# Four one-bank PSUM tiles become one tile of four banks, copied out by one ScalarE instruction a unit

## The chip, the core and the metric

The kernel runs on one core of one Trainium2 chip. A core has five engines with an instruction queue each: TensorE (PE in the profile, with its weight loads shown as PEld), VectorE (DVE), ScalarE (ACT), GpSimd (POOL) and SyncE (SP). The last two mostly issue DMAs here. Matrix products land in PSUM, which has eight banks of 512 float32 per partition. Every queue runs in order, and an instruction that needs another engine's result waits on that engine's semaphore. The metric is the time of one execution on the device in microseconds (us); lower is better.

## What is computed

The reference is one block with two halves, on `x` of 2048 x 576. Everything that the change touches is in the first half, a long convolution whose kernel is made on the chip:

```
h = _layernorm(x) * (1 + ca) + sa
logdA = dt * A;  P = exp(logdA[:, :, None] * l)
K = einsum("dn,dnl,dn->dl", Cc, P, dB).real
y = irfft(rfft(pad(u)) * rfft(pad(K)))[:L] + u * Dskip
x = x + ga * y
h = _layernorm(x) * (1 + cb) + sb
x = x + gb * (z1 * (w_sp @ layernorm(z2) + b_sp)) @ w_out
```

The second half is a gated MLP with a 2048 x 2048 mixing product.

## The kernel before

**Two phases.** The convolution (`ssm`) fills about the first 340 us of the span, the first layer normalisation of the MLP follows, and from about 400 us on TensorE works through the MLP's products without a pause. The convolution works in small units, each a generator: a step issues some instructions and yields. `ORDER`, a list of 1336 steps such as `e30` or `z16` (a letter for the kind of unit, a number for which one), says which unit takes its next step. Instructions are tied to that order on every engine's queue: `Pin` passes each of them through `keep_in_program_order`.

**Units that matter here.** `M` (`mod_unit`) makes the modulation rows; `A` (`ln_half`, 16 units) forms the first transform of the normalised input in four banks and copies it to `st1o`; `e`, `t`, `p`, `k` make the convolution kernel for a group of channels (`e` writes tiles `et`, `t` writes `ft`, `p` writes `pg`, `k` writes `kab`); `1` (`k1_unit`, 36 units, steps such as `115` for unit 15) transforms it in two banks and copies it to the tiles shown as `k_a` and `k_b`; `u` transforms the input into `uu`; `z` (`z_unit`, 36 units) multiplies the two: its first instruction is a VectorE product that reads a bank directly (`zz<-pk,uu`); `v` (`v_unit`, 36 units) transforms back in two banks and copies to `v`; `y` forms the output rows, and its VectorE sum also reads a bank.

**PSUM.** Four banks belong to two tiles `ps` of two banks each. The other four are four tiles of one bank, `pk_a` to `pk_d`, handed out by `ps1()`; the digits of `PLAN["pk"]` say which tile each request gets. A unit that needs two or four banks asks two or four times, and copies each bank out with a ScalarE instruction of its own: 4 x 128x288 in `ln_half`, 2 x 128x256 in `k1_unit` and `v_unit`, 2 x 128x288 in `mod_unit`. TensorE may write a bank again as soon as the copy of that one bank has ended.

**Waits.** The framework keeps instructions apart by tile: an instruction waits for earlier ones, on other engines, that touched the same tile. With four separate tiles this is a wait by bank.

Of the kernel before, what the change touches and what calls it, by code (L numbers as in the profile page):

```python
# [9 lines left out]
F32 = mybir.dt.float32  # L10
# [3 lines left out]
AF = mybir.ActivationFunctionType  # L14
# [16 lines left out]
COPIED = set()  # L31
# [6 lines left out]
    "pk": "01230123230123012301230120123012301231023102310232102130213021302130213021302301230122301230123012312031203120"  # L38
        "31203120312031203103201320323012302310231023103210321031203120132012031231201230123012032012031203120321021021"
        "30230123013021032103210321321031021032130130213021320123120312012301230123023102310231032103210123012301230213"  # L40
        "021320312031230123012310312031203120312031320120312031203123013021300101010101010101010101010101010101010101",
# [13 lines left out]
B0 O0 O0 O0 O0 B2 O0 O0 O0 O0 B7 O0 B1 O0 O0 O0 B6 O0 O0 O0 O0 O0 O0 x0 O0 O0 O0 O0 P0 S0 O0 S0 B3 O0 O0 i2 O0 O0 O0 P0 M2 O0 O0 S0 S0 B4 P0 S0 O0 Q0 P0 e1 S0 M2 e1 i1 e0  # L55
P0 P0 g0 e1 e0 P0 e0 e1 P0 t1 t2 i0 g1 O0 M2 e0 P0 M1 t1 t2 t1 P0 P0 t0 w3 P0 M1 t0 M2 t1 t0 t2 M1 M0 M1 M0 t0 e2 j1 R1 P0 p1 M3 t2 M0 p1 M3 R0 e2 R3 e6 p1 M0 B5 e2 M0 e6
M3 w4 k1 e4 e2 P0 M3 k1 O0 P0 e3 11 p0 e4 11 e6 M4 M0 e5 p0 P0 p0 e6 S1 S1 p2 M4 k0 M4 p2 11 R2 p2 e5 k0 e5 S1 M0 M3 M0 P0 k2 M4 e5 M0 P0 t5 k2 A0 e3 A0 S1 A0 A0 A0 w5 t5
S1 e3 P0 e3 A0 t3 S1 A1 t5 A1 A1 r2 A1 P0 t3 R4 A1 t7 A0 R5 A1 A2 A2 O0 P0 t3 t3 A2 A2 t4 P0 A1 A2 A2 A3 p3 A2 A3 t5 P0 r3 A3 A3 t4 t4 j2 M4 10 10 e4 A3 A3 A3 e4 12 p3 12
e7 p3 e7 P0 e7 R7 t7 10 R6 P0 p5 S2 12 k3 e8 e7 O0 k3 e8 A4 S2 A4 S2 A4 e8 S2 A4 A4 A4 e8 p5 P0 A5 t4 A5 A5 P0 A5 p5 A5 p4 A5 t7 a4 A4 A5 t6 A6 A6 A6 p4 A6 t6 A6 p4 A6 t8
A7 A7 P0 t7 A7 A7 O0 k4 A6 P0 S2 A7 13 t6 p7 A7 k4 t8 p7 R9 14 13 O0 k5 P0 P0 a5 t6 14 14 t8 p7 Q1 13 t8 M5 x3 k7 P0 e11 R8 A7 k5 M5 S3 k7 S3 A8 A8 e11 R11 e9 A8 e10 e11  # L60
P0 e9 e11 P0 p6 S3 S3 A8 P0 A8 R10 t10 A8 e10 A9 t10 A9 A9 A9 p8 p8 r6 e10 A9 A9 t9 e10 t10 A10 A8 P0 A10 A10 A10 A9 t11 p6 A10 A10 17 P0 t10 M5 p6 17 k6 M5 p8 t11 t9 17
k6 A11 A11 r7 S3 t11 t11 e12 A11 A11 Q2 15 R13 A11 A11 A10 p11 k8 t9 15 15 R12 A11 k8 A12 p11 A12 e12 A12 p11 A12 e14 A12 t14 A12 A13 e14 p10 A13 t14 A13 R15 e9 p10 A13
p10 A13 R14 A13 e9 t14 A12 e12 t12 e12 A14 A14 t9 A14 t15 A14 A14 t12 A13 t14 A14 t12 A15 A15 t14 O0 O0 A15 e16 k10 P0 A15 P0 A15 16 A15 P0 O0 p9 t12 k11 16 M5 p9 A14 A15
p9 C0 16 t14 18 c1 k10 f0 18 110 k11 18 110 e14 U2 110 U1 U0 t15 p12 111 t15 111 z2 111 t15 u2 t16 p12 u2 U5 p12 u0 e14 k9 c0 z2 z2 u0 k9 t16 k12 U4 p14 u1 19 U14 t16 U7
e16 k12 e15 19 t16 19 U23 e13 e15 e15 e16 u1 e15 c3 u7 e16 e13 p14 u4 u7 e13 u4 p14 c2 p15 z1 z1 e13 t13 U29 v2 u14 U6 t16 v2 p15 z4 U10 u14 t13 u6 t13 p15 t18 k15 z4 u6
u5 t16 k15 z1 p16 t18 p16 u29 e18 u5 U15 v1 z0 t13 u29 t18 e17 X1 t18 v1 U3 e18 115 115 u10 v1 v2 z0 u10 z0 X3 p16 e17 115 k14 k14 u3 b1 e17 e22 u3 p13 U12 e22 t17 e17
e18 112 e18 p13 e22 z4 p13 112 t22 t17 v0 e22 t22 t22 z6 112 z6 v0 U13 t17 z5 v4 k13 v4 t22 t17 z5 114 Q3 z6 k13 v0 114 p17 u15 e19 p17 t22 v6 p17 t19 u15 k16 z5 t18 t19
v6 114 t18 113 p18 113 113 k16 z3 v5 z3 p18 v6 u13 k17 t19 t22 v5 p18 U11 z7 e20 t19 u13 116 k17 e19 U9 z7 p22 k18 116 u23 k18 116 117 e20 v4 117 e20 p22 117 z7 p22 e23
t20 v7 z3 u23 t20 v5 z15 t20 z15 U18 v7 u12 e23 t24 e20 b0 v7 t20 z15 e19 e23 e26 u12 v3 e19 e23 v15 e26 p19 v3 t23 v3 v15 z14 u9 z9 p19 t20 t23 U16 u9 z10 p19 z14 v15
u11 t24 z9 t20 z14 u16 t24 z9 t23 U19 u11 u16 t23 k19 v14 e24 U17 p20 k19 e21 v14 e24 v9 z10 p20 v9 k22 p23 u17 119 t26 e21 t21 u17 e24 119 U8 e26 p23 k22 119 p20 e24 p23  # L70
t21 e21 e26 e21 z12 122 v9 t24 z12 t26 k20 122 W1 122 t21 u8 k20 y1 t26 y1 t21 U20 z12 k23 120 W3 u8 t26 k23 t25 120 120 y1 t26 p21 v12 123 p21 v12 z8 u18 t26 v12 z10 123
123 t24 p21 u19 z8 u18 z11 t24 k21 u19 t25 e32 U24 z8 v14 t25 k21 t25 v8 p24 y3 e25 v8 U21 p24 u20 z11 y3 X0 U28 118 e32 p26 z13 v8 118 p26 118 u20 e25 v10 v10 t28 e28
z11 z13 p24 v11 W0 p26 e28 e25 e28 t30 v11 z13 y0 e28 121 e25 t28 121 t30 k26 k24 121 t28 e32 k26 k24 y0 e30 U31 e32 e30 v11 v13 t30 e27 e30 t28 v13 t30 z16 z20 p25 U25
z16 v13 e30 124 v10 u25 t30 y3 124 u28 124 z20 t30 z17 t27 t28 p25 z20 p25 z16 t27 u28 u25 v20 k25 z17 t28 p30 v20 v16 t27 k25 t31 W4 126 v16 t27 z17 X4 126 p30 y0 e27
z19 y4 u21 e29 126 z19 y4 u21 p30 U22 v20 e29 v17 v16 e27 e29 y4 e33 v17 p28 e27 e29 k30 t31 p27 p27 k30 z19 X7 e33 125 125 p27 X2 u31 z23 t29 125 u31 t31 v19 k27 W7 z23
v19 t29 130 p28 t31 y7 k27 W2 130 u24 y7 z21 t29 p28 W6 z21 e31 130 e34 k28 t29 e33 u24 p29 e31 z21 v17 e31 u22 k28 e33 p29 y2 y2 e31 e34 p29 v21 y7 t34 v19 e35 u22 128
v21 t34 128 k29 128 p31 k29 U26 127 e35 e34 t34 127 e35 z23 e35 v21 e34 t33 X6 t34 p31 127 t32 v23 p31 U30 v23 129 z22 129 129 z18 t33 z22 k31 z18 u30 z18 u26 t34 t34 t33
k31 u30 y6 u26 131 t32 t35 131 U33 v18 131 y2 v23 z22 p34 y6 t32 v22 v18 t33 U35 v22 y6 U27 z29 p34 t32 u27 p34 z27 u27 z29 U32 u33 X8 v22 t35 t32 u33 U34 k34 z27 p33 t35
v29 k34 v18 p33 t32 v29 z27 134 X5 p33 W8 134 z28 t35 134 u34 u35 u34 z28 v27 u35 p35 v28 v27 p35 k33 z24 W11 v29 p35 v28 z31 p32 z24 z31 k33 133 133 k35 k35 y8 p32 v31
y8 133 p32 v27 z26 k32 z24 v31 135 k32 z26 132 z26 135 135 132 v24 v28 132 v31 W5 z34 v24 v26 D0 z35 L2 v26 v24 z34 L4 y5 v34 z35 L9 v34 y5 y8 L3 z25 z30 y5 L7 v35 z25  # L80
z25 u32 v35 u32 v25 z30 v25 L10 X19 L13 X11 v30 v26 L0 X17 X12 v25 z32 v30 L11 L20 v30 z33 z32 v32 X9 z33 v32 v33 v33 v34 W9 L12 L6 L1 v32 L14 v33 X13 y11 X10 X16 W13 y11
v35 y9 y13 W12 W10 W14 y12 L15 W16 y10 y13 L8 W17 L18 y12 y11 X14 W15 X15 W18 y9 y9 W19 y10 L19 y16 y16 y17 L22 y14 X18 y17 y15 y19 y18 y14 y12 y10 y15 y19 L16 y15 L17
y18 y16 y13 y17 y19 y14 y18
# [112 lines left out]
class Rings:  # L196
# [7 lines left out]
    def __call__(self, pool, shape, dt, name, bufs):  # L204
        if name not in self.plan:
            return pool.tile(shape, dt, name=name, bufs=bufs)
        if name not in self.tiles:
            self.tiles[name] = [pool.tile(shape, dt, name=f"{name}_{chr(97 + i)}", bufs=1) for i in range(bufs)]
        i = self.at[name]
        self.at[name] = i + 1  # L210
        return self.tiles[name][self.plan[name][i]]


class Pin:
# [5 lines left out]
    def __getattr__(self, name):  # L220
        f = getattr(self.engine, name)

        def call(*a, **k):
            return self.tc.keep_in_program_order(f(*a, **k))  # L224

        return call

# [9 lines left out]
def ssm(tc, I, x1_d, consts_s, dram, mod_d, mlp):  # L237
# [6 lines left out]
    with ExitStack() as ctx:  # L244
# [12 lines left out]

        def ps1():
            return ring(psp, [128, 512], F32, "pk", 4)
# [178 lines left out]
        def mod_unit(k):  # L438
            wm = wmt.pop(k)
            pm = [ps1(), ps1()]  # L440
            for hh in range(2):
                for kt in range(6):
                    j = (kt + 2 * hh) % 4
                    T.matmul(pm[hh][32 * j:32 * j + 32, :HC], ec[:, kt:kt + 1].to_broadcast([96, 32]),
                             wm[hh][:, kt], start=kt < 4, stop=kt >= 2, skip_group_check=True)
            yield
            mpart = ep.tile([128, D], F32, name="mpart", bufs=1)
            for hh in range(2):
                A.activation(v3(mpart)[:, hh], pm[hh][:, :HC], AF.Copy)
            yield  # L450
            pm = [ps1(), ps1()]
            for hh in range(2):
                T.matmul(pm[hh][:, :HC], ones, mpart[:, HC * hh:HC * hh + HC], start=True, stop=True)
            yield
            src = [t[:, :HC] for t in pm]
            if k == 2:
                for hh in range(2):
                    A.activation(v3(gar)[:, hh], src[hh], AF.Copy)
            elif k == 1:
                for hh in range(2):  # L460
                    V.scalar_tensor_tensor(v3(cga)[:, hh], src[hh], 1.0, v3(gar)[:, hh], op0=ALU.add, op1=ALU.mult)
# [2006 lines left out]
```

## Time and profile before

| | |
|---|---|
| median of three runs | 1696.31 us (1691.14 to 1697.28) |
| profiled execution | 1691.0 us, of which the span from first to last instruction is 1688.9 us |
| ScalarE in the span | 873.8 us busy, 1307 instructions |
| VectorE in the span | 1298.4 us busy, 2241 instructions |
| granted TensorE clock | 0.99 on average |

The page gives busy times by engine, the share of each engine in 40 slices, the DMA queues, the chain of work that ended last and the costliest groups. For a change in one stage the table by windows (busy time of each engine between two moments) and the timeline (each instruction with its start and length) say more than the page's averages. A row of the timeline reads: start, length, engine, line, operation, output<-input, partitions x elements; in brackets how long the engine had been idle before it and what ended that.

### The profile page before, as it was taken

What the parts mean: (1) busy time and instruction counts of PE and PEld (TensorE: products, weight loads), DVE (VectorE), ACT (ScalarE), POOL (GpSimd) and SP (SyncE); (2) the same over time, 40 slices, a digit from 0 to 9 for tenths busy, and PEclk for the clock granted to TensorE, in tenths of its full rate; (3) what the DMA queues carried; (4) which work ended last, traced back from release to release, by engine and by line L of the source; (5) the groups of instructions that cost most, each with busy time, mean ns of one, the idle gap of its engine ahead of it and who ended that gap; (6) DMA issues with size and microseconds to landing.
All of it is one profiled execution on the core that took longest, in us unless ns stands there. A gap on an engine that the chain in (4) does not pass through costs nothing.

```text
span 1688.9 us, 39922 instructions
## 1 busy us (share of the span) xinstructions
PE 1615.6 (96%) x16868; PEld 1235.7 (73%) x16868; DVE 1298.4 (77%) x2241; ACT 873.8 (52%) x1307; POOL 209.7 (12%) x340
## 2 busy tenths in 40 slices
PE   3778999989999999999999999999999999999999
PEld 1344677755555557778878888888888888888887
DVE  7898999867989877988997776894443487787555
ACT  6889999675776664555444433342321133353221
POOL 3251111112222110000000000000111100111100
PEclk9978999999999999999999999999999999999999
DMA  9667645596888898776738887664667573777560
GB/s 231 170 215 229 203 140 176 171 317 208 280 287 243 251 261 297 242 270 234 249 118 302 282 292 257 219 218 166 232 213 243 189 221 121 275 281 252 189 241 29
DMA packets 186402, 380.61 MB, mean 225 GB/s; under 512 B 38464, under 2 KB 105792, under 8 KB 185456
## 3 DMA queue, kind: packets, MB, share of 16 engines
q1 hardware_dynamic: 145216, 182.10, 35.2%
q0 software_dynamic: 34528, 169.11, 30.1%
q10 hardware_dynamic: 6480, 26.86, 3.9%
q8 instruction: 132, 2.16, 0.5%
q14 instruction: 46, 0.38, 0.1%
HBM read 272.73 MB, written 105.29 MB: 224 GB/s over the span
## 4 chain that ended last, share of the span: by engine, by line
PE 77%; DVE 7%; DMA 3%; issue 2%; ACT 2%; SPq 0%; POOL 0%; ACTq 0%; DVEq 0%; POOLq 0%
PE ps L224 58%; PE pz L224 10%; PE pk_b L224 2%; PE pk_a L224 2%; DMA zset<-set_d 2%; PE pk_c L224 2%; PE pk_d L224 1%; DVE zset L224 1%; DVE gt L224 1%; DVE bsz L224 1%; PE ps_a L224 0%; PE ps_b L224 0%; DMA v_d<-v_a 0%; PE pt L224 0%; DMA uu_a<-in_x 0%
## 5 line engine op out<-in xcount | busy, mean ns | idle before, releaser
L224 PEld LDWEIGHTS <-zset 128*128 128x128 f16 x7182 | 702.2, 98 | 86.5 <-DMA zset<-set_d 2.0
L224 PE MATMUL ps<-wsp,zset 128*128 128x256 f16 x6048 | 666.8, 273 | 2.2 <-DMA zset<-set_d 1.1
L224 PE MATMUL pz<-wz,nt 128*128 128x512 f16 (+1 forms) x1120 | 220.8, 358 | 1.5 <-ACT nt L224 1.0
L224 ACT ACTIVATE z<-gt 128x1024 f16<-128x1024 f32 x56 | 59.0, 1054 | 250.4 <-DVE gt L224 250.4
L224 PEld LDWEIGHTS <-nt 128*128 128x128 f16 x1120 | 109.4, 98 | 107.1 <-ACT nt L224 1.5
L2164 POOL DMA_DIRECT2D zset<-set_d x96 | 50.8, 529 | 862.5 <-PE ps L224 619.7
L224 PE MATMUL ps<-wout,z 128*128 128x288 f16 x1092 | 138.4, 286 | 0.0
L224 DVE SCALAR_TENSOR_TENSOR gt<-ps,sc,bsp 128x512 f32<-128x512 f32 x36 | 27.0, 749 | 143.0 <-PE ps L224 141.3
L224 PEld LDWEIGHTS <-z 128*128 128x128 f16 x1176 | 115.1, 98 | 28.9
L224 DVE TENSOR_TENSOR raw<-raw 128x256 f32<-128x256 f32 (+3 forms) x238 | 126.8, 539 | 7.7 <-DMA raw<-z_d 3.5
L224 PE MATMUL ps<-n2o,zset 128*128 128x256 f16 x1134 | 128.2, 273 | 0.0
L224 DVE SCALAR_TENSOR_TENSOR gt<-ps,sc,gt 128x512 f32<-128x512 f32 (+1 forms) x180 | 122.2, 696 | 7.6
L224 ACT ACTIVATE zset<-raw 128x1792 f16<-128x1792 f32 x48 | 81.1, 1691 | 59.3 <-PE ps L224 21.6
L224 DVE TENSOR_TENSOR zset<-raw,zset 128x1792 f16<-128x1792 f32 x48 | 96.9, 2020 | 15.7 <-ACT zset L224 15.7
L224 DVE TENSOR_TENSOR z<-ps,z 128x512 f32<-128x512 f32 (+1 forms) x126 | 72.0, 599 | 32.3 <-ACT z L224 25.9
L224 ACT ACTIVATE z<-pz,sc 128x512 f32<-128x512 f32 (+1 forms) x96 | 51.9, 574 | 39.9 <-PE pz L224 32.7
L224 ACT ACTIVATE wsp<-raw,sc 128x1792 f16<-128x1792 f32 x25 | 44.5, 1783 | 46.2 <-DVE raw L224 40.2
L224 ACT ACTIVATE z<-z,sc 128x1024 f32<-128x1024 f32 x21 | 24.1, 1148 | 76.0 <-DVE z L224 72.3
L224 ACT ACTIVATE z1b<-gt 128x512 f16<-128x512 f32 (+1 forms) x22 | 17.7, 821 | 84.0 <-DVE gt L224 84.0
L224 PE MATMUL ps<-n2q,wf 128*128 128x512 f16 x252 | 55.7, 379 | 0.0
L224 DVE BATCH_NORM_STATS2 bsz<-z 128x6 f32<-128x384 f32 x96 | 48.4, 548 | 5.0 <-ACT z L224 4.4
L224 DVE SCALAR_TENSOR_TENSOR wsp<-raw,sc,wsp 128x1792 f16<-128x1792 f32 x25 | 52.0, 2078 | 0.3 <-ACT wsp L224 0.3
(793 smaller groups left out, 2772.0 us busy)
## 6 DMA issues: line engine op xcount, KB each, us to landing
zset<-set_d POOLq DMA_DIRECT2D x96, 896.0 KB, 5.2
raw<-z_d SPq DMA_DIRECT2D x48, 512.0 KB, 5.6
set_d<-zset ACTq DMA_DIRECT2D x24, 896.0 KB, 6.4
z_d<-z POOLq DMA_DIRECT2D x32, 576.0 KB, 8.2
zset<-wa_d POOLq DMA_DIRECT2D x18, 896.0 KB, 4.9
raw<-in_w_spT SPq DMA_DIRECT2D x25, 512.0 KB, 4.4
set_d<-zset SPq DMA_DIRECT2D x12, 896.0 KB, 5.8
wst<-in_w_in SPq DMA_DIRECT2D x8, 1024.0 KB, 9.3
```

The source lines that it names most:

```text
L224: return self.tc.keep_in_program_order(f(*a, **k))
L2164: self.nc.gpsimd.dma_start(o, self.set_d[f, j - 1] if j else self.wa_d[f])
```

## The change

The four tiles become one tile `banks` of 128 x 4 x 512. `ps1()` returns one bank of it, and a new `psn(n)` returns n neighbouring banks. `PLAN["pk"]` is a new list of digits, so that a unit's banks lie side by side. Each unit of two or four banks then issues one copy for all of them. This takes 130 ScalarE instructions away (48 in `ln_half`, 36 each in `k1_unit` and `v_unit`, 10 in `mod_unit`) and 2 VectorE ones. The lines of `ORDER` are wrapped at other places, but its 1336 steps are the same. TensorE's, GpSimd's and SyncE's instructions and their order are the same too.

One tile for all four banks would make the framework keep every reader of `banks` apart from every writer. `Pin.apart` takes that back between TensorE and the two readers: for each product written, and each read, it declares that there is no dependence on recent accesses by the other side to other banks. `READS` holds the reads of both ScalarE and VectorE, and `WRITES` those of TensorE. Between a read by ScalarE and a read by VectorE nothing is declared.

```
+    def apart(self, done, aps):
+        b = {x for ap in aps for x in banks_of(ap)}
+        if b:
+            names = {ap.tensor.name for ap in aps if hasattr(ap, "tensor")} - {ap.tensor.name for ap in aps if banks_of(ap)}
+            ins = getattr(done, "ins", done)
+            mine, others = (WRITES, READS) if self.engine is self.tc.nc.tensor else (READS, WRITES)
+            for c, i, n in others:
+                if not b & c and not names & n:
+                    self.tc.declare_no_dep(ins, i, reason="another bank")
+            mine.append((b, ins, names))
+        return done
...
+READS, WRITES = deque(maxlen=48), deque(maxlen=320)
...
+        banks = psp.tile([128, 4, 512], F32, name="banks", bufs=1)
+
         def ps1():
-            return ring(psp, [128, 512], F32, "pk", 4)
+            return banks[:, ring.take("pk")]
+
+        def psn(n):
+            i = min([ring.take("pk") for _ in range(n)])
+            return banks[:, i:i + n]
...
         def ln_half(k):
-            pms = [ps1() for _ in range(4)]
+            pms = psn(4)
...
-            for g, pm in enumerate(pms):
-                A.activation(o[:, g], pm[:, :HC], AF.Copy)
+            A.activation(o, pms[:, :, :HC], AF.Copy)
+            for _ in range(4):
                 yield
...
         def k1_unit(g):
-            pm = [ps1(), ps1()]
+            pm = psn(2)
...
-            for h in range(2):
-                pk = pm[h][:, :256].rearrange("p (c k) -> p k c", c=8)
-                if (g, h) in COPIED:
-                    V.tensor_copy(o[:, :, h], pk)
-                else:
-                    A.activation(o[:, :, h], pk, AF.Copy)
-                yield
+            A.activation(o, pm[:, :, :256].rearrange("p h (c k) -> p k h c", c=8), AF.Copy)
+            yield
+            yield
...
         def v_unit(n):
-            pm = [ps1(), ps1()]
+            pm = psn(2)
...
-            for q in range(2):
-                A.activation(v[:, 256 * q:256 * q + 256], pm[q][:, :256], AF.Copy)
+            A.activation(v.rearrange("p (q d) -> p q d", q=2), pm[:, :, :256], AF.Copy)
```

What this makes of the queues shows at three places. The first is ScalarE's queue in the first stage, where `ln_half` unit 3 is copied to `st1o_b` and the first `k1` units to `k_a`. Before, the four copies of a unit are taken apart by other work:

```order
L224 ACTIVATE st1o_b<-pk_c 128x288
L224 ACTIVATE st1o_b<-pk_d 128x288
L224 ACTIVATE ft_b<-ps_b 128x1024
L224 ACTIVATE k_a<-pk_c 128x32x8
L224 ACTIVATE st1o_b<-pk_b 128x288
L224 ACTIVATE st1o_b<-pk_a 128x288
L224 ACT_TABLE_LOAD
L224 ACTIVATE et_a<-pk_c 128x512
L224 ACTIVATE k_a<-pk_b 128x32x8
L224 ACTIVATE et_d<-ps_b 128x1024
L224 ACTIVATE k_a<-pk_d 128x32x8
```

The same place in the changed kernel:

```order
L227 ACTIVATE st1o_b<-banks 128x1152
L227 ACTIVATE ft_b<-ps_b 128x1024
L227 ACTIVATE k_a<-banks 128x32x16
L227 ACT_TABLE_LOAD
L227 ACTIVATE et_a<-banks 128x512
L227 ACTIVATE k_a<-banks 128x32x16
L227 ACTIVATE et_d<-ps_b 128x1024
```

The whole copy stands where the first part stood, and the later parts have moved ahead of what stood between.

The second place is ScalarE's queue where, in the profiled execution of before, about 260 us have passed: the second half of `e30` (`et_e`), a load of a function table, `k1` unit 24 (`k_b`). Each row names the semaphores it waits for: `PE_49`, `DVE_49` and `Activation_49` count the instructions that those engines have ended, `DMASW` and `DMAHW` the DMAs. Before:

```order
L224 ACTIVATE et_e<-ps_b 128x1024 [waits DVE_49,PE_49]
L224 ACTIVATE v_a<-pk_a 128x256 [waits DMASW5_49,PE_49,Activation_49]
L224 ACTIVATE v_a<-pk_c 128x256 [waits DVE_49,PE_49,Activation_49]
L224 ACTIVATE et_e<-pk_b 128x512 [waits PE_49]
L224 ACT_TABLE_LOAD
L224 ACTIVATE ft_a<-ft_a 128x1024 [waits DVE_49]
L224 ACTIVATE k_b<-pk_c 128x32x8 [waits PE_49]
L224 ACTIVATE k_b<-pk_b 128x32x8 [waits PE_49]
L224 ACTIVATE ft_a<-ft_a,consts_s 128x1024
```

In the changed kernel:

```order
L227 ACTIVATE et_e<-ps_b 128x1024 [waits PE_49]
L227 ACTIVATE v_a<-banks 128x512 [waits DMASW5_49,PE_49,Activation_49]
L227 ACTIVATE et_e<-banks 128x512 [waits DVE_49]
L227 ACT_TABLE_LOAD
L227 ACTIVATE ft_a<-ft_a 128x1024
L227 ACTIVATE k_b<-banks 128x32x16 [waits PE_49]
L227 ACTIVATE ft_a<-ft_a,consts_s 128x1024
```

The two halves of `v_a` and of `k_b` have become one row each, and the second row of `et_e` waits for VectorE now. By the count that it waits for, the awaited instruction is the product of unit `z16` (`zz_a<-banks,uu_f`), which reads bank 2; `et_e` reads bank 3.

The third place is VectorE's queue at the same time, with the products of units `z16` and `z20`. Before:

```order
L224 TENSOR_TENSOR pg_a<-et_a,ft_b 128x1024 [waits PE_49]
L224 TENSOR_TENSOR zz_a<-pk_d,uu_f 128x1024 [waits PE_49,Activation_49]
L224 TENSOR_TENSOR zz_b<-pk_a,uu_b 128x1024 [waits PE_49,Activation_49]
L224 TENSOR_TENSOR pg_a<-et_a,ft_b 128x1024
L224 TENSOR_TENSOR zz_b<-zz_b 128x256 [waits DVE_49]
```

In the changed kernel:

```order
L227 TENSOR_TENSOR pg_a<-et_a,ft_b 128x1024 [waits PE_49]
L227 TENSOR_TENSOR zz_a<-banks,uu_f 128x1024 [waits PE_49,Activation_49]
L227 TENSOR_TENSOR zz_b<-banks,uu_b 128x1024 [waits Activation_49]
L227 TENSOR_TENSOR pg_a<-et_a,ft_b 128x1024
L227 TENSOR_TENSOR zz_b<-zz_b 128x256 [waits DVE_49]
```

The rows stand as before, but the counts differ. Before, `z20` waited for an earlier copy out of its own bank; now it waits for the whole copy of `k_b` above, which reads banks 1 and 2, while `z20` reads bank 0. Over the whole program 34 such waits of ScalarE for a VectorE read of another bank, and 35 of VectorE for a ScalarE read of another bank, are in the changed kernel, and none in the kernel before. All but four stand among the `z` and `y` units, from about 160 us on. TensorE waits for ScalarE at 185 places where it did at 333 (counting its accesses to these banks), always for a reader of the same bank or tile.

More of the change, by code (lines that the diff above doesn't have):

```diff
@@ L1 @@
 import math
+from collections import deque
 from contextlib import ExitStack
@@ new lines @@
+v12 123 p21 v12 z8 u18 t26 v12 z10 123 123 t24 p21 u19 z8 u18 z11 t24 k21 u19 t25 e32 U24 z8 v14 t25 k21 t25 v8 p24 y3 e25 v8 U21 p24 u20 z11 y3 X0 U28 118 e32 p26 z13
+v8 118 p26 118 u20 e25 v10 v10 t28 e28 z11 z13 p24 v11 W0 p26 e28 e25 e28 t30 v11 z13 y0 e28 121 e25 t28 121 t30 k26 k24 121 t28 e32 k26 k24 y0 e30 U31 e32 e30 v11 v13
+t30 e27 e30 t28 v13 t30 z16 z20 p25 U25 z16 v13 e30 124 v10 u25 t30 y3 124 u28 124 z20 t30 z17 t27 t28 p25 z20 p25 z16 t27 u28 u25 v20 k25 z17 t28 p30 v20 v16 t27 k25
@@ L84 @@
+v34 z35 L9 v34 y5 y8 L3 z25 z30 y5 L7 v35 z25 z25 u32 v35 u32 v25 z30 v25 L10 X19 L13 X11 v30 v26 L0 X17 X12 v25 z32 v30 L11 L20 v30 z33 z32 v32 X9 z33 v32 v33 v33 v34
+W9 L12 L6 L1 v32 L14 v33 X13 y11 X10 X16 W13 y11 v35 y9 y13 W12 W10 W14 y12 L15 W16 y10 y13 L8 W17 L18 y12 y11 X14 W15 X15 W18 y9 y9 W19 y10 L19 y16 y16 y17 L22 y14 X18
+y17 y15 y19 y18 y14 y12 y10 y15 y19 L16 y15 L17 y18 y16 y13 y17 y19 y14 y18
 """
@@ L208, in __call__, with take @@
             self.tiles[name] = [pool.tile(shape, dt, name=f"{name}_{chr(97 + i)}", bufs=1) for i in range(bufs)]
+        return self.tiles[name][self.take(name)]
+    def take(self, name):
         i = self.at[name]
         self.at[name] = i + 1
-        return self.tiles[name][self.plan[name][i]]
+        return self.plan[name][i]
 class Pin:
@@ L223, in call, with banks_of @@
         def call(*a, **k):
-            return self.tc.keep_in_program_order(f(*a, **k))
+            return self.apart(self.tc.keep_in_program_order(f(*a, **k)), a + tuple(k.values()))
         return call
+    def apart(self, done, aps):
[10 more added lines that the diff above has]
+READS, WRITES = deque(maxlen=48), deque(maxlen=320)
+def banks_of(ap):
+    t = getattr(ap, "tensor", None)
+    if t is None or not t.name.startswith("banks"):
+        return ()
+    at = {ap.offset % 2048}
+    for step, n in list(ap.ap)[1:]:
+        at = {o + step * j for o in at for j in (range(n) if step >= 512 else (0, n - 1))}
+    return {o // 512 for o in at}
 class Pinned:
@@ L447, in mod_unit @@
             mpart = ep.tile([128, D], F32, name="mpart", bufs=1)
+            A.activation(v3(mpart), pm[:, :, :HC], AF.Copy)
+            yield
+            pm = psn(2)
             for hh in range(2):
-                A.activation(v3(mpart)[:, hh], pm[hh][:, :HC], AF.Copy)
+                T.matmul(pm[:, hh, :HC], ones, mpart[:, HC * hh:HC * hh + HC], start=True, stop=True)
             yield
-            pm = [ps1(), ps1()]
-            for hh in range(2):
-                T.matmul(pm[hh][:, :HC], ones, mpart[:, HC * hh:HC * hh + HC], start=True, stop=True)
-            yield
-            src = [t[:, :HC] for t in pm]
+            src = pm[:, :, :HC]
             if k == 2:
-                for hh in range(2):
-                    A.activation(v3(gar)[:, hh], src[hh], AF.Copy)
+                A.activation(v3(gar), src, AF.Copy)
             elif k == 1:
-                for hh in range(2):
-                    V.scalar_tensor_tensor(v3(cga)[:, hh], src[hh], 1.0, v3(gar)[:, hh], op0=ALU.add, op1=ALU.mult)
+                V.scalar_tensor_tensor(v3(cga), src, 1.0, v3(gar), op0=ALU.add, op1=ALU.mult)
             elif k == 0:
-                for hh in range(2):
-                    V.tensor_tensor(v3(sga)[:, hh], src[hh], v3(gar)[:, hh], op=ALU.mult)
+                V.tensor_tensor(v3(sga), src, v3(gar), op=ALU.mult)
                 yield
@@ L473, in mod_unit @@
                 mrow = mpart if k == 4 else ep.tile([128, D], F32, name="gar", bufs=1)
-                for hh in range(2):
-                    if k == 4:
-                        A.activation(v3(mrow)[:, hh], src[hh], AF.Identity, bias=one)
-                    else:
-                        A.activation(v3(mrow)[:, hh], src[hh], AF.Copy)
+                if k == 4:
+                    A.activation(v3(mrow), src, AF.Identity, bias=one)
+                else:
+                    A.activation(v3(mrow), src, AF.Copy)
                 yield
@@ L548, in ln_half @@
                         rows = slice(32 * g, 32 * g + 32)
-                        T.matmul(pms[g][64 * t:64 * t + 64, :HC], x[rows], y[rows, c], start=st, stop=not st, skip_group_check=True)
+                        T.matmul(pms[64 * t:64 * t + 64, g, :HC], x[rows], y[rows, c], start=st, stop=not st, skip_group_check=True)
                 yield
             o = ring(ep, [128, 4, HC], F32, "st1o", 2)
-            for g, pm in enumerate(pms):
-                A.activation(o[:, g], pm[:, :HC], AF.Copy)
+            A.activation(o, pms[:, :, :HC], AF.Copy)
+            for _ in range(4):
                 yield
@@ L660, in k1_unit @@
                         s = slice(64 * h, 64 * h + 64)
-                        T.matmul(pm[h][64 * ri:64 * ri + 64, 64 * i:64 * i + 64], kk[s, i], r1[ri][s, s], start=True, stop=True,
+                        T.matmul(pm[64 * ri:64 * ri + 64, h, 64 * i:64 * i + 64], kk[s, i], r1[ri][s, s], start=True, stop=True,
                                  skip_group_check=True)
@@ L750, in v_unit @@
                     rows = slice(64 * q, 64 * q + 64)
-                    T.matmul(pm[q][:, :256], m[rows], zz[rows, k, 256 * r:256 * r + 256], start=not t, stop=t == len(terms) - 1,
+                    T.matmul(pm[:, q, :256], m[rows], zz[rows, k, 256 * r:256 * r + 256], start=not t, stop=t == len(terms) - 1,
                              skip_group_check=True)
```

70 lines of the change are left out of this document (31 added, 39 removed).

## Prediction

> **What bounds the kernel now.** I read the windows first, since one stage alone is changed, then the timelines of the two engines that empty PSUM.
>
> ```profile
> core 0: us, PE busy (x) PEld busy (x) DVE busy (x) ACT busy (x) POOL busy (x), PEclk, DMA share, GB/s
> 60.00:158.00 98.00, 75.42 (x1695) 41.31 (x1693) 89.08 (x165) 90.62 (x183) 39.37 (x62) 0.83 0.63 196
> 158.00:335.00 177.00, 171.97 (x3960) 126.39 (x3960) 170.40 (x218) 159.53 (x279) 25.90 (x43) 1.00 0.59 176
> ...
> 340.00:360.00 20.00, 16.69 (x202) 13.54 (x198) 14.45 (x34) 14.74 (x25) 3.29 (x6) 1.00 1.08 335
> ...
> 400.00:450.00 50.00, 50.00 (x271) 26.46 (x269) 46.65 (x142) 35.97 (x57) 11.04 (x15) 1.00 0.74 228
> ```
>
> From 400 us on TensorE is full and nothing of its work changes, so whatever the convolution gains or loses moves the end by as much. From 60 to 158 us ScalarE (92%) and VectorE (91%) lead; from 158 to 335 us three engines are nearly full: TensorE idles 5.0 us of 177, VectorE 6.6, ScalarE 17.5. From 340 us the DMA engines are full. A stage with so little idle time gains little when one engine is relieved, and loses at once when one engine is held.
>
> **Fewer copies.** The timeline of ScalarE shows what a copy costs in a row of copies:
>
> ```profile
> 208.47 0.38 ACT L224 ACTIVATE k_a<-pk_c 128x256 f32<-128x256 f32 x1
> 208.75 0.38 ACT L224 ACTIVATE k_a<-pk_a 128x256 f32<-128x256 f32 x1
> 209.02 0.60 ACT L224 ACTIVATE uu_h<-pk_b 128x512 f32<-128x512 f32 x1
> 209.49 1.05 ACT L224 ACTIVATE ft_b<-ps_a 128x1024 f32<-128x1024 f32 x1
> 210.40 0.42 ACT L224 ACTIVATE v_a<-pk_c 128x256 f32<-128x256 f32 x1
> 210.66 0.44 ACT L224 ACTIVATE v_a<-pk_a 128x256 f32<-128x256 f32 x1
> ```
> ```profile
> 100.45 0.39 ACT L224 ACTIVATE st1o_b<-pk_a 128x288 f32<-128x288 f32 x1
> 100.74 0.40 ACT L224 ACTIVATE st1o_b<-pk_c 128x288 f32<-128x288 f32 x1
> ```
>
> A 128x256 copy lasts about 0.40 us, but the next begins 0.26 us after its start: their ends overlap. A 128x512 one takes the queue for 0.47 us and a 128x1024 one, across two banks, for 0.91. That is 0.84 ns for an element and some 0.045 us for an instruction. Two copies of 256 made one save 0.05 us, and four of 288 (0.29 each, 1.16) against one of 1152 (0.045 + 0.97 = 1.01) save 0.15. So 72 x 0.047 + 16 x 0.15 + 10 x 0.05 gives 6.3 us of ScalarE: 3.8 before 158 us (`ln_half`, `mod_unit` and half of `k1_unit`) and 2.5 after. By lengths (four 0.43 us copies against one of about 1.15, two of 0.40 against 0.61, two of 0.42 against 0.67) it would be 24.5 us, the upper bound; the lower is nothing. I take 6.3, the distance of starts being what a full queue pays. The Trainium skill ("ScalarE: Activation LUTs", What ACT_TABLE_LOAD costs) gives 186 ns + 0.833 ns an element, and about 93 ns of overlap: 130 x 0.093 = 12 us. The length of 0.40 agrees; the overlap here is 0.13 us, so I stay with the rows. Of the 3.8 us before 158 us I let half reach the end, as VectorE is as full: **-2** (0 to -3.8). The 2.5 after it go into the next part.
>
> **Copies that hold banks longer.** TensorE's waits from 60 to 158 us show that banks are short there:
>
> ```profile
> PE pk_a L224 <- ACT st1o_b L224: 2.4, 2, 1.8
> PE pk_c L224 <- ACT st1o_b L224: 2.2, 3, 1.3
> ```
>
> The first bank of an `ln_half` unit came free after 0.43 us and will after 1.15, 0.72 later, 16 times: 0 to +11.5 us. The last comes free 0.15 earlier (1.30 against 1.15), and in this stage TensorE idles a quarter of the time and ScalarE has other work in its queue. I take 0. The other end stays in the range. The new digits of the plan leave as many steps between a copy and the next use of its bank as before or more, so I count nothing for them.
>
> **New waits between ScalarE and VectorE.** This decides. In the changed program a copy by ScalarE waits for the VectorE read of `banks` that stands ahead of it in the list of steps, and a VectorE read for the copy ahead of it, whatever the banks: 34 and 35 waits that did not exist. They cost nothing where the two queues pass these points in the order of the list, but the list was free to run them past each other. The place at 260 us:
>
> ```profile
> 261.50 0.62 ACT L224 ACTIVATE et_e<-pk_b 128x512 f32<-128x512 f32 x1
> 262.14 1.28 ACT L224 ACT_TABLE_LOAD   x1
> 263.43 1.06 ACT L224 ACTIVATE ft_a<-ft_a 128x1024 f32<-128x1024 f32 x1
> 264.39 0.37 ACT L224 ACTIVATE k_b<-pk_c 128x256 f32<-128x256 f32 x1
> 264.66 0.38 ACT L224 ACTIVATE k_b<-pk_b 128x256 f32<-128x256 f32 x1
> ```
> ```profile
> 262.56 1.22 DVE L224 TENSOR_TENSOR zz_a<-pk_d,uu_f 128x1024 f32<-128x1024 f32 x1 [1.65 <-PE pk_d L224]
> 263.70 1.22 DVE L224 TENSOR_TENSOR zz_b<-pk_a,uu_b 128x1024 f32<-128x1024 f32 x1
> 264.84 1.22 DVE L224 TENSOR_TENSOR pg_a<-et_a,ft_b 128x1024 f32<-128x1024 f32 x1
> ```
>
> `et_e` began at 261.50, and now has to wait for the end of `z16` at 263.78: +2.28. Behind it stand the table load, `ft_a` and `k_b`, which moves from 264.39 to 266.67 and, 0.61 long, ends at 267.28. `z20` began at 263.70 and now waits for that: +3.58 on VectorE, with `pg_a` and all later products queued behind it. So each engine holds the other in turn.
>
> I compared start and end at each crossing of the two timelines from `z2` to the last `y` before 341 us. In 32 of them the awaited instruction ended after the waiting one had begun: 17 on VectorE, 17.9 us in sum, and 15 on ScalarE, 23.4 us. The first and the last before 335 us:
>
> ```profile
> 160.38 1.22 DVE L224 TENSOR_TENSOR zz_a<-pk_a,uu_a 128x1024 f32<-128x1024 f32 x1
> ...
> 332.52 1.23 DVE L224 TENSOR_TENSOR zz_b<-pk_b,uu_h 128x1024 f32<-128x1024 f32 x1 [2.10 <-PE pk_b L224]
> ```
> ```profile
> 161.34 0.60 ACT L224 ACTIVATE et_c<-pk_b 128x512 f32<-128x512 f32 x1
> ...
> 333.90 0.38 ACT L224 ACTIVATE kab_b<-pk_c 128x256 f32<-128x256 f32 x1 [1.83 <-PE pk_c L224]
> ```
>
> They are 161.94 - 160.38 = 1.56 and 334.28 - 332.52 = 1.76 us. The sums overlap, since a late engine no longer has to wait for the other; so I carried two delays, a for ScalarE and d for VectorE, from crossing to crossing: where VectorE waits, d becomes at least a plus the shortfall there, and where ScalarE waits, a at least d plus its own. At the last crossing before 335 us d is 31 us if neither catches up, and 18 if every idle moment of both (the 17.5 and 6.6 us above) goes into catching up. The first is too much, the second too little, because most idle moments were waits for TensorE, which comes later too when its inputs do. I take the middle, 24.5, less the 2.5 us that ScalarE saves there: **+22** (15 to 31).
>
> **The tail.** From 340 us on loads of `v_d` and of the MLP's weights share full DMA engines.
>
> ```profile
> wst<-in_w_in SPq DMA_DIRECT2D x2, 1024.0 KB, 11.4
> ```
>
> Weight loads need none of the late results. If they get out of the way in time, the last stretch is shorter: those 2 MB and 1 MB in smaller ones take 10 us at the 335 GB/s of the row at 340 us. They stand in one queue with loads that have to wait, so I take **-4** (0 to -10).
>
> **Sum.** -2 + 0 + 22 - 4 = +16 us on the profiled execution's 1691.0, 1707. The median of the runs shown stands 5.3 us above it, so I predict 1712. 0.5% of it is 8.5 us, about what a measurement can tell from no change.
>
> **Rivals.** *The waits are absorbed.* If the relieved ScalarE runs ahead and the crossings fall into the list's order by themselves, only the two savings remain, -2 to -6, and the tail cannot shrink: about 1692. For it: ScalarE has 17.5 us idle and the waits reorder the queues only by 1 to 3 us. Against it: VectorE has 6.6 us idle and is held 17.9 by starts alone. 0.17.
>
> *ScalarE is the bound and instructions cost their length.* Then up to 24.5 us leave its queue, but VectorE's work stays and it idles 8.9 + 6.6 us from 60 to 335 us, so at most some 13 us reach the end: 1683 to 1687. Against it stand the overlapping starts. 0.05.
>
> *TensorE slows down as well.* The windows show its clock at 0.83 where it was 77% busy and at 1.00 where it was 97% busy. With 22 us more, the stage to 335 us would be 86% busy, between these; at 0.92 its 172 us would take 15 us more: about 1727. 0.14. The Trainium skill ("TensorE: Matmul & The Clock Gate", What's actually happening) halves the clock after an idle window of about 3.4 us; single holds here are 1 to 3.6 us. By that rule the cost would come in pieces, as the rows above, a mean of 0.83, allow.
>
> *The copies are not the changed thing*, because the one tile makes TensorE wait for other banks too: its waits point to readers of its own bank, so 0.02, and about 1735.
>
> **How the numbers follow.** The forecast has 0.62, with 1703 to 1722 as its own range. The range reaches down to the sum of the low ends (15 - 3.8 - 10 = +1, 1697) and up into the slower clock, with the held banks: 1697 to 1731. Slower by over 0.5% is above 1704.8: nearly all of the forecast and the two slow rivals, 0.77. Below 1687.8: the second rival and a little of the first, 0.06. Between: 0.17.
>
> **What would show it.** Right: ScalarE's instructions fall by 130 but its busy time by 5 to 10 us only; rows of `zz` and `xb` on VectorE with ScalarE as the releaser of the idle time, and copies (`et`, `uu`, `v`, `k`) on ScalarE with VectorE as theirs, some 30 us in all between 160 and 340 us, where before there was almost none; the `z` stage 15 to 25 us longer, and the MLP as long as before. Wrong: the two waits for each other sum to a few us, or the first stage to 158 us changes by more than 5 us either way, or the MLP from 400 us on changes its length.

## The result and the profile after

The changed kernel takes 1737.72 us (median of four, 1735.83 to 1740.60) against 1696.80 before: a ratio of 1.0249, 95% interval 1.0222 to 1.0277. The forecast of slower was right and its size was not: +41 us by medians where +16 was predicted. The profiled execution took 1735.8 us, 44.8 more than that of before, of which the span is 1733.9.

| | before | changed |
|---|---|---|
| ScalarE busy, instructions | 873.8 us, 1307 | 870.4 us, 1177 |
| VectorE busy, instructions | 1298.4 us, 2241 | 1300.0 us, 2239 |
| granted TensorE clock | 0.990 | 0.980 |
| first `z` product starts | 160.38 us | 169.78 us |
| last crossing of the prediction (`zz_b` of `uu_h`) starts | 332.52 us | 374.67 us |

The same two VectorE instructions that the prediction quoted as the first and the last of their stage, in the timeline of the changed kernel:

```profile
169.78 1.23 DVE L227 TENSOR_TENSOR zz_a<-banks,uu_a 128x1024 f32<-128x1024 f32 x1 [1.83 <-ACT et_c L227]
...
374.67 1.22 DVE L227 TENSOR_TENSOR zz_b<-banks,uu_h 128x1024 f32<-128x1024 f32 x1 [5.80 <-ACT kab_b L227]
```

So, of the 44.8 us between the two profiled executions, 9.4 were lost ahead of the `z` units, 32.8 more between the two instructions (called the `z` stage from here on), and from there to the end 2.7. The windows of the changed kernel, cut at these two instructions (start:end, length, busy time of each engine with its instructions, granted clock, DMA share, GB/s):

```profile
60.00:169.78 109.78, 79.43 (x1757) 46.09 (x1752) 90.65 (x167) 89.73 (x121) 38.53 (x60) 0.77 0.60 187
169.78:374.67 204.89, 175.79 (x3844) 125.25 (x3844) 167.69 (x212) 154.72 (x220) 24.93 (x43) 0.97 0.49 144
```

And before, cut at the same two instructions:

```profile
60.00:160.38 100.38, 77.55 (x1715) 42.39 (x1713) 91.42 (x168) 92.98 (x187) 39.37 (x62) 0.83 0.64 199
160.38:332.52 172.14, 167.58 (x3822) 123.34 (x3822) 165.93 (x212) 156.23 (x272) 24.11 (x42) 1.00 0.59 174
```

VectorE does the same 212 instructions in the second stretch and is busy for as long (167.7 against 165.9 us), but the stretch is 32.8 us longer: VectorE waits. TensorE's busy time grows by 8.2 us (for 3844 matmul records against 3822) with its clock at 0.97. The waits of the changed kernel from 160 to 380 us (engine, tile written, awaited engine and tile: us in total, times, longest), VectorE's first:

```profile
DVE zz_b L227 <- ACT k_b L227: 5.8, 2, 3.5
DVE zz_b L227 <- ACT kab_b L227: 5.8, 1, 5.8
...
DVE zz_a L227 <- ACT v_a L227: 4.1, 2, 2.9
DVE xb_a L227 <- ACT kab_b L227: 3.1, 2, 2.2
```

ScalarE's, from the same view:

```profile
ACT kab_b L227 <- DVE zz_b L227: 4.0, 1, 4.0
ACT v_a L227 <- DVE zz_b L227: 3.2, 1, 3.2
ACT v_b L227 <- DVE zz_b L227: 2.7, 2, 2.5
ACT v_a L227 <- DVE zz_a L227: 2.4, 1, 2.4
ACT et_e L227 <- DVE zz_a L227: 2.3, 1, 2.3
```

Summed over all rows of the view, VectorE waits 32.2 us for ScalarE there (7.6 in the same window of before, of which 0.6 lie in the `z` stage of before) and ScalarE 28.6 for VectorE (0.6 before). The place at 260 us that the prediction worked out lies at 285 us now:

```profile
285.93 0.60 ACT L227 ACTIVATE et_e<-banks 128x512 f32<-128x512 f32 x1 [2.26 <-DVE zz_a L227]
286.55 1.28 ACT L227 ACT_TABLE_LOAD   x1
287.84 1.06 ACT L227 ACTIVATE ft_a<-ft_a 128x1024 f32<-128x1024 f32 x1
288.80 0.58 ACT L227 ACTIVATE k_b<-banks 128x512 f32<-128x512 f32 x1
```

VectorE at the same time:

```profile
284.67 1.23 DVE L227 TENSOR_TENSOR zz_a<-banks,uu_f 128x1024 f32<-128x1024 f32 x1
289.41 1.22 DVE L227 TENSOR_TENSOR zz_b<-banks,uu_b 128x1024 f32<-128x1024 f32 x1 [3.52 <-ACT k_b L227]
```

`et_e` sat idle for 2.26 us and `z20` for 3.52, where the crossing of the two old timelines gave 2.28 and 3.58. The two agree so well because both engines come to this place about 22 us later than before, so that it is the old crossing, shifted.

### The profile page after: what moved, and what is told of

It reads as the page before. It is cut to its first block, busy times and chain, and to the rows that moved or that the text cites. A ratio compares the mean times of both kernels' runs of the same rounds, so it can differ in the third digit from the quotient of the medians.

```text
span 1733.9 us, 39690 instructions
## 1 busy us (share of the span) xinstructions
PE 1627.1 (94%) x16868; PEld 1241.5 (72%) x16868; DVE 1300.0 (75%) x2239; ACT 870.4 (50%) x1177; POOL 209.8 (12%) x340
## 4 chain that ended last, share of the span: by engine, by line
PE 71%; DMA 4%; DVE 4%; issue 1%; ACT 0%; SPq 0%; POOL 0%; ACTq 0%; DVEq 0%; POOLq 0%
PE ps L227 56%; PE pz L227 12%; DMA zset<-set_d 2%; PE banks L227 1%; DVE zset L227 1%; DMA v_d<-v_a 1%; DVE gt L227 1%; PE pt L227 1%; DMA v_d<-uu_d 0%; DMA uu_a<-in_x 0%; SPq L227 0%; DVE wout L227 0%; DVE zz_b L227 0%; DVE raw L227 0%; DVE ot L227 0%
## 5 line engine op out<-in xcount | busy, mean ns | idle before, releaser
L227 DVE TENSOR_TENSOR z<-ps,z 128x512 f32<-128x512 f32 (+1 forms) x126 | 72.0, 599 | 32.2 <-ACT z L227 25.8
```

The lines of the kernel that those rows point to most:

```text
L227: return self.apart(self.tc.keep_in_program_order(f(*a, **k)), a + tuple(k.values()))
```

## The experiments

Every ratio is against runs of the kernel before on the same chip. All kernels are edits of the changed kernel.

**The waits taken away.** The reads of the other reading engine are declared independent too, where they touch other banks:

```
-            for c, i, n in others:
+            if mine is READS:
+                others = [*WRITES, *[x for x in READS if x[3] is not self.engine]]
+            for c, i, n, e in others:
...
-            mine.append((b, ins, names))
+            mine.append((b, ins, names, self.engine))
```

> The changed kernel, in which reads by ScalarE and reads by VectorE of different banks are declared independent of each other too: the 69 waits between the two engines for reads of other banks are gone, nothing else is changed. In the changed kernel the first z product came 9.4 us later than before and the last one before 335 us came 42.2 us later. Theory A (two causes: the new waits in the z stage, and banks held longer by the merged copies in the stage ahead of it): the first z product stays 9 us late, the z stage is as long as before within 3 us, and the time is 1700 to 1710 us. Rival B (the merged copies of two banks hold TensorE up in the z stage too, and the waits between the two engines only show it): the z stage stays 15 us or more longer, above 1718 us. Rival C (the new waits are behind it all, the stage ahead included): 1690 to 1698 us.

Measured: 1710.44 us, ratio 1.0085 (1.0056 to 1.0115), 27 us below the changed kernel. The `z` stage is 180.22 us long, 24.7 less than with the waits:

```profile
170.00:350.22 180.22, 168.02 (x3824) 120.97 (x3824) 167.03 (x212) 154.90 (x221) 24.09 (x42) 1.00 0.55 164
```

So the waits are most of the loss, rivals B and C fall, and 14 us stay by medians. In the profiled executions, which stand 20 us apart, the first `z` product is 9.6 us late, as theory A had it, and the `z` stage 8.1 us longer than before, which it had not.

**Copies apart at their old steps.** Four copies again in `ln_half`, with the waits (first kernel) and without (second); in a third, also without the waits, `k1` and `v` likewise:

```
-            A.activation(o, pms[:, :, :HC], AF.Copy)
-            for _ in range(4):
+            for g in range(4):
+                A.activation(o[:, g], pms[:, g, :HC], AF.Copy)
                 yield
...
-            A.activation(o, pm[:, :, :256].rearrange("p h (c k) -> p k h c", c=8), AF.Copy)
-            yield
-            yield
+            for h in range(2):
+                A.activation(o[:, :, h], pm[:, h, :256].rearrange("p (c k) -> p k c", c=8), AF.Copy)
+                yield
```

> The changed kernel, but the copy of four banks in ln_half is four copies of one bank again, at the steps where they stood before; the 69 waits stay. Theory A: the stage ahead of the z units is back to its old length (first z product within 2 us of before), the z stage stays some 33 us longer, the time is 1726 to 1732 us. If the plan's new digits or the k1 copies hold that stage up, the first z product stays 6 to 9 us late and the time is 1735 to 1740 us.

> Both edits: no waits for reads of other banks, and ln_half copied out bank by bank; k1, v and mod units keep their merged copies. Theory A: both losses are gone, and what the 72 merged copies of k1 and v save shows, 1690 to 1697 us. If the two causes aren't independent, or a third one is there (the plan, or the merged copies of two banks), it stays above 1702 us.

> As the one with both edits, and the copies of k1 and v are two of one bank each again: what is left of the change is the one tile and the plan's new digits (and the mod units). Theory A: no change from before, 1693 to 1700 us, and 1 to 5 us slower than with the merged k1 and v copies. If the new digits cost something, above 1702 us. If merged copies of two banks cost time by holding banks, this one is faster than with them.

Measured: 1732.23 us (1.0216, 1.0181 to 1.0252) with the waits, 1709.34 (1.0073, 1.0045 to 1.0101) without them, and 1707.72 (1.0074, 1.0048 to 1.0100) with those of `k1` and `v` apart as well. They have a flaw that the expectations did not see: the new digits hand a bank on as soon as the step of the merged copy has passed, so parts copied at later steps read a bank into which another unit's products have already gone, and wait for those. So they show little: with all these copies apart some 11 us stay, which points away from the merging as the whole of the rest, but the extra waits blur it.

**One tile alone, without and with the waits.** The old digits and all old copies, on one tile of four banks (`pm` is a list of single banks, as before the change); the second kernel lacks the declaration between readers:

```
-            i = min([ring.take("pk") for _ in range(n)])
-            return banks[:, i:i + n]
+            return [banks[:, ring.take("pk")] for _ in range(n)]
```

> The kernel before with nothing but its four tiles made one tile of four banks: old digits, every bank copied out by itself at its old step, and reads of different banks by ScalarE and VectorE declared independent. So far: the changed kernel 41 us above before, and 14 us above it once the 69 waits are gone. What makes up these 14 us is open. Theory P (the plan's new digits give units banks that come free later) and theory M (a merged copy holds banks longer): 1692 to 1701 us. Theory T (one tile by itself costs time, by other waits than those): 1705 us and more.

> The same without that declaration, so one tile with its 71 waits between ScalarE and VectorE for reads of other banks, old digits and old copies. If the cost of the waits doesn't depend on the merged copies and the digits, 24 to 30 us above the run without them: 1720 to 1728 us. If ScalarE's smaller load absorbs part of it in the changed kernel, more, above 1730 us; if the merged copies make the waits longer, less, 1705 to 1718 us.

Measured: 1696.87 us, ratio 0.9990 (0.9975 to 1.0005), and 1731.54 us, 1.0211 (1.0187 to 1.0236). One tile costs nothing. The waits alone cost 35 us, more than the 27 that they cost in the changed kernel. The expectation had a reason ready for that (ScalarE's smaller load absorbs part of them in the changed kernel); that the other losses there cover some of theirs is as possible, and no run tells the two apart. The `z` stage without and with the waits, in profiled executions 5 and 8 us above their medians:

```profile
161.83:339.08 177.25, 170.52 (x3824) 125.91 (x3824) 166.21 (x212) 156.92 (x272) 24.20 (x42) 0.98 0.57 171
```
```profile
165.24:372.86 207.62, 179.12 (x3834) 128.49 (x3834) 167.63 (x211) 157.27 (x271) 25.03 (x43) 0.97 0.48 143
```

**Digits and copies apart.** First the old digits with merged copies wherever they give neighbouring banks:

```
+            if pm.whole is not None:
+                A.activation(o, pm.whole[:, :, :256].rearrange("p h (c k) -> p k h c", c=8), AF.Copy)
+            else:
+                for h in range(2):
+                    A.activation(o[:, :, h], pm[h][:, :256].rearrange("p (c k) -> p k c", c=8), AF.Copy)
```

> One tile, no waits for reads of other banks, old digits, and merged copies wherever these digits give neighbouring banks: all 16 of ln_half, 22 of 36 of k1, 17 of 34 of v, 5 of 7 of mpart; the other units copy bank by bank, both copies at the first step. Theory P: the 14 us are gone, 1690 to 1700 us. Theory M: most of them stay, since all copies of four banks and over half of those of two are here, 1704 to 1710 us.

Then the new digits with the copies of `ln_half`, `k1` and `v` apart, but all at the step of the merged one (shown for `k1`):

```
-            A.activation(o, pm[:, :, :256].rearrange("p h (c k) -> p k h c", c=8), AF.Copy)
+            for h in range(2):
+                A.activation(o[:, :, h], pm[:, h, :256].rearrange("p (c k) -> p k c", c=8), AF.Copy)
             yield
             yield
```

> The changed kernel without the 69 waits, with the new digits, and with the copies of ln_half, k1 and v taken apart again, bank by bank, all at the step where the merged copy stands. Theory M: banks come free one after the other again, 1694 to 1701 us. Theory P: 1706 to 1714 us, as with merged copies, plus up to 6 us for ScalarE's 120 further instructions.

Measured: 1701.56 us (1.0031, 1.0017 to 1.0045) with old digits and merged copies; 1707.99 us (1.0064, 1.0047 to 1.0081) with new digits and none merged. Both causes are there: against the 1696.87 us of one tile with the old digits and every copy apart, the merged copies cost 4.7 us, and the new digits 11 with the copies apart (which here stand at the step of the merged one, so the 11 us hold that shift too). The two shares do not simply add up: against the kernel without the waits (1710.44 us), which has the new digits and all copies merged, taking the copies apart wins only 2.5 us. TensorE's waits from 165 to 335 us in the kernel with one tile and old digits:

```profile
PE ps_b L227 <- issue: 2.5, 2, 2.0
PE ps_a L227 <- DVE pg_b L227: 2.0, 1, 2.0
PE banks L227 <- issue: 1.7, 2, 1.2
PE banks L227 <- DVE zz_b L227: 0.2, 1, 0.2
```

And with new digits and every copy apart:

```profile
PE banks L227 <- DVE zz_a L227: 3.5, 4, 1.6
PE banks L227 <- issue: 2.9, 2, 1.9
PE banks L227 <- ACT uu_c L227: 1.8, 1, 1.8
PE banks L227 <- ACT kab_b L227: 0.8, 1, 0.8
PE ps_b L227 <- issue: 0.6, 1, 0.6
PE banks L227 <- ACT k_b L227: 0.6, 1, 0.6
```

Its waits for banks sum to 10.8 us against 1.9 (the smallest rows are left out above), and a third of them is for a `z` product. Which requests these are can be worked out on the timeline of before, by setting each request's first matmul against the end of the read that frees the bank which the new digits give it. A unit's copies are taken as the one merged copy for this, or the old digits, whose timeline it is, would have no such place at all. From 158 to 335 us 29 requests come too early, by 16.1 us in sum; with the old digits 15, by 3.2. The largest are `u12` (1.76, the bank of `z15`), `133` (1.73, of `z31`) and `u8` (1.49, of `z12`). In the kernel without the waits two of these three stand in TensorE's timeline, as the matmuls of `u12` and `u8`, 13 and 14 us later than before:

```profile
223.90 1.08 PE L227 MATMUL banks<-u_c,small 128*64 128x256 f32 x8 [1.64 <-DVE zz_a L227]
...
247.33 1.08 PE L227 MATMUL banks<-u_d,small 128*64 128x256 f32 x8 [1.23 <-DVE zz_a L227]
```

**Digits of our own.** A search over digits that keep a unit's banks side by side, for the smallest such sum, gives 3.2 us from 158 to 335 us, as the old digits have. It was used without the waits and with all copies merged, then with `ln_half` apart at its old steps (as in the diff further below), then with `k1` and `v` apart as well (as in the diff above).

> The changed kernel without the 69 waits, all copies merged, but with other digits: neighbouring banks as before, chosen so that on the timeline of before each request gets the banks that came free longest ago. By that timeline, from 158 to 335 us the new digits hand out a bank too early by 16 us in sum (29 places), the old ones by 3 us (15 places) and these by 3 us; from 60 to 158 us all three are alike. So far: 14 us above before with the new digits. Theory P (the digits cost some 10 us in the z stage): 1697 to 1703 us, like the old digits with merged copies (1701.6), and TensorE's waits for banks from 165 to 335 us down from 10 to under 4 us. Rival (the 14 us lie in the copies, and the old digits did better because a third of the copies was not merged there): 1706 us or more.

> As the run before, and ln_half copied out bank by bank at its old steps (digits chosen anew for that); the copies of k1, v and mod stay merged. By the timeline of before, merged copies of four banks hand banks out too early by 13.5 us in sum from 60 to 158 us, single ones by 3. Theory (merging four banks costs 4 to 8 us ahead of the z stage, merging two saves some 2.5 us of ScalarE's queue and holds nothing): 1690 to 1696 us, the first z product within 2 us of before. If merging two banks costs as much as it saves: 1696 to 1700 us. If the copies of ln_half have no part: as the run before.

> As the run with ln_half apart, but the copies of k1 and v are two of one bank each as well, both at the step of the merged one. The difference is what 70 merged copies of two banks are worth: by starts 0.047 us each, 1.6 us of ScalarE ahead of the z units and 1.7 in them, so 0 to 3.5 us slower than with them; by lengths 0.19 us each, up to 13 us slower; faster if holding the second bank longer costs time.

Measured: 1707.47 us (1.0073, 1.0055 to 1.0092), 1700.65 (1.0031, 1.0015 to 1.0047) and 1701.14 (1.0023, 1.0006 to 1.0040). The first two missed, and all three are slower than they should be, by a fault in the digits: two requests that the MLP makes at 342 and 359 us had been forgotten, so that from there on units got the digits meant for others, and banks still in use. Up to the `z` product that starts at 345.9 us in the kernel with one tile alone, the second of them is 1.1 us later than that kernel; by the product at 358.9 us it is 5.7 us later. The pair of the second and third still tells something, as both have the fault: with the 72 copies of two banks in `k1` and `v` (the expectations say 70) merged or apart, the time is the same within some 4 us, so the forecast by starts (0 to 3.5 us) held and the one by lengths (up to 13) did not. Then the digits with those two requests counted:

```
-    "pk": "01230123230123012013012013012301230012301230123012013201230012301230123023012013012300123001230123001230120123"
+    "pk": "01230123230123010231230123012301230012301230123013120301230012301230123023013120012300123001230123001230120123"
...
```

> As the run with other digits and all copies merged, but with digits that count the two requests of the MLP's scales (at 342 and 359 us) too; in the last run of that kind these two shifted all later digits by one or two, which cost some 5 us after 345 us and gave units from there on the wrong banks. Theory: the digits cost 7 to 10 us, so this is 1700 to 1704 us, and what is left above before is the copies of four banks, with the first z product 5 to 8 us late against the run with one tile alone. If copies of four banks cost nothing: 1695 to 1698 us. If the digits aren't the cause: 1707 us and more.

and with the copies of `ln_half` apart:

```
-            pms = psn(4)
+            pms = [ps1() for _ in range(4)]
...
-            A.activation(o, pms[:, :, :HC], AF.Copy)
-            for _ in range(4):
+            for g, pm in enumerate(pms):
+                A.activation(o[:, g], pm[:, :HC], AF.Copy)
                 yield
```

> The same with ln_half copied out bank by bank at its old steps (its digits chosen for that). Theory: no loss is left, 1692 to 1697 us, 3 to 8 us below the run with the merged copies of four banks; by starts, the 70 merged copies of two banks can be worth at most 3 us against before. If more than 1700 us, one of the remaining parts (merged copies of two banks, these digits) costs time too.

Measured: 1704.23 us, ratio 1.0039 (1.0020 to 1.0057), and 1697.23 us, ratio 1.0000 (0.9983 to 1.0018). The first differs from the kernel without the waits in its digits alone: 6 of the 14 us are gone, TensorE's waits for banks from 165 to 335 us fall from 10.3 to 5.0 us, and the `z` stage from 180.22 to 174.15. With the four-bank copies apart (and digits that suit them) 7 more are gone. Each of these medians is known to 3 to 5 us, so the 6 and the 7 are rough. The first `z` product shows the second step: in the kernel with all copies merged and in the one with `ln_half` apart,

```profile
170.14 1.23 DVE L227 TENSOR_TENSOR zz_a<-banks,uu_a 128x1024 f32<-128x1024 f32 x1 [1.37 <-ACT uu_a L227]
```

and

```profile
163.81 1.22 DVE L227 TENSOR_TENSOR zz_a<-banks,uu_a 128x1024 f32<-128x1024 f32 x1
```

What is left in the last kernel, 72 merged copies of two banks and those of `mod_unit`, neither costs nor brings anything that can be measured; no version here is faster than before.

## Why the prediction was wrong in size

The 41 us, by medians: the waits 27 (1737.7 to 1710.4), the new digits 6 (to 1704.2), the merged copies of four banks 7 (to 1697.2), the merged copies of two banks and the one tile 0. These shares belong to the order in which the parts were taken away; in another order the digits have 11 and the merged copies 2.5 to 4.7.

Of the prediction's own signs, the 130 instructions less and the releasers of the waits came as it said. The waits of the two engines for each other sum to some 60 us where it said 30, the `z` stage is 32.8 us longer where it said 15 to 25, and the stage ahead of it is 9.4 us longer, beyond the 5 us that it named as a sign of being wrong. Step by step:

- **New waits between ScalarE and VectorE: right in mechanism, and the largest term, 5 us too small.** The two waits worked out at 260 us came within 0.06 us. Forecast +22 with 15 to 31 as bounds; shown 27 in this kernel and 35 without its other losses. In the `z` stage, for which the prediction worked out 18 to 31 and took the middle, 24.5, the waits cost 24.7 in this kernel and 30.4 where they stand alone. So how much the engines catch up depends on what else holds them, and is not settled here. In this kernel hardly any idle moment was used for it: VectorE and ScalarE together wait for TensorE 27.0 us in that stage, against 25.9 without the new waits. Where these stand alone it is 15.9 against 22.8.
- **The digits: this step failed.** "The new digits of the plan leave as many steps between a copy and the next use of its bank as before or more, so I count nothing for them." That looked at distances as a whole. The sum of the places that are too early tells more, and there the new digits have 16.1 us against 3.2. Shown cost: 6 with merged copies, 11 without, where nothing was counted.
- **Copies that hold banks longer: this step failed too.** Taken as 0 with 0 to +11.5 as bounds; measured 7 between the last two kernels, and 4.7 for all merged copies with the old digits. The first stage did not hide that the first of the four banks comes free later: the first row of TensorE's waits on `ln_half` (60 to 165 us) is, in the changed kernel,

```profile
PE banks L227 <- ACT st1o_b L227: 12.4, 7, 2.9
```

  where the four rows for `st1o_b` before sum to 7.3. On one tile with the old digits, TensorE's waits for all `st1o` copies in that window are 7.7 us with every copy apart and 14.7 with the four-bank copies merged. The argument that TensorE idles a quarter of the time there did not hold; by which of these waits the delay reaches the stage's end is not shown.
- **Fewer copies: -2 and -2.5 did not show.** ScalarE's busy time fell by 3.4 us, less than the 5 to 10 named as a sign. Apart or merged, the 72 copies of two banks give the same time (1701.14 and 1700.65, and 1697.23 against 1696.87 for one tile with nothing merged); a gain of 2 or 3 us would be hidden in the scatter. The estimate by starts was much nearer than that by lengths, 24.5 us; the Trainium skill ("Perfetto Trace Analysis", Optimizing Scalar/DVE Operations) gives some 51 ns of overhead for a ScalarE access to PSUM, and the 0.045 us of the prediction's rows lie close to it.
- **The tail: -4 did not come.** The MLP's first products on the chain of work that ended last start, before and changed, at

```profile
385.78 9.24 PE pz L224 x42
```
```profile
430.60 9.24 PE pz L227 x42
```

  which is 53.3 us behind the last crossing before and 55.9 now; from there to the end both kernels take 1303 us, so the MLP kept its length, as forecast. In between, the chain of the changed kernel runs through transfers to `v_d`, as that of before does, one behind the other:

```profile
387.76 7.21 DMA v_d<-v_a
...
395.95 5.28 DMA v_d<-v_a
...
402.75 7.20 DMA v_d<-uu_d
```

  and the DMA engines are as full there as they were: the window from 405 to 425 us has a share of 1.05, and the prediction's row at 340 us 1.08. The weight loads themselves were not followed; what shows is that the stretch did not become shorter.
- **The rivals.** That the waits are absorbed is refuted. That TensorE slows down as well came true in part: its clock was 0.97 in the `z` stage, with 8.2 us more busy time. Without the waits it is 1.00 in that stage, but 0.98 on one tile alone, also without them (both rows stand in the experiments); how much of the loss it carries is not shown. That the copies bound the kernel by their length is refuted by the pair with the 72 copies apart. That one tile makes TensorE wait for other banks had the time nearest to the measured one, 1735, but by luck: one tile alone takes 1696.87 us.

What made the range too narrow is that two costs that were counted as nothing came out at 6 and 7 us; with them the forecast of 1712 would have been 1725, with 27 for the waits 1730, and without the 4 us for the tail and the 2 for fewer copies in the first stage 1736. The range was also narrower than the prediction's own bounds: its low end sums all the low ends, but the high ends, 0 + 11.5 + 31 + 0 = +42.5, would have reached 1739.

## What to carry to other kernels

Where several banks share one tile, look at every pair of engines that touches it: leaving the waits in place between two readers cost 35 us here, and declaring reads of different banks independent brought it back to nothing; the Trainium skill ("PSUM — Partial Sum Buffer", PSUM bank collisions raise a hardware error) asks for an order between two engines only within one bank and quadrant. The order by bank is what the kernel at 0.9990 of before keeps. When a table of buffers is changed, sum up the requests that come too early on a measured timeline, one by one, and take no mean. Merging copies can pay at most what the starts of instructions in a full queue say, 0.05 us each, and here not even that showed; the 16 merged copies of four banks cost some 5 to 7 us, and TensorE's waits for those copies grew by as much.

## What was not expected

In the stage ahead of the `z` units TensorE stands still for some time behind the first matmul into a bank that a `k1` copy has just freed, with no releaser in the profile. In the changed kernel:

```profile
110.70 0.21 PE L227 MATMUL banks<-dsk,small 128*32 128x4 f32 x1
113.83 0.23 PE L227 MATMUL banks<-dsk,small 128*32 128x4 f32 x4 [2.92 <-issue]
```

It is 4.55 us in the kernel without the waits and between 0.7 and 3.3 in seven of the others with the new digits or our own; in two of these, and in all three with the old digits on one tile, it does not show at this matmul. The trace's DMA records hold a hint. The instruction queue q8 moves packets of 16 KB, 132 of them in the changed kernel for TensorE's 33,887 matmuls and weight loads, some 256 each. In all nine kernels with this stop, such a packet lands 1.0 to 1.5 us before the stop ends (here at 112.49 us). So TensorE may have waited for its next instructions; no run was made for it, and its cause stays open.

The second concerns the clock. In the `z` stage of the changed kernel it averages 0.97, where it was 1.00 before, although this is the longest single stop of TensorE there (2.6 us, the last number):

```profile
PE banks L227 <- ACT v_a L227: 3.0, 2, 2.6
```

The Trainium skill ("TensorE: Matmul & The Clock Gate", What's actually happening) speaks of an idle window of about 3.4 us; in this stage stops of up to 2.6 us went with a lower clock. The trace's clock records show it as pieces of 3.4 and 6.8 us at half clock; the first two begin at 205.1 and 297.2 us, where the two longest stops (2.5 and 2.6 us) end.
